# Transposed activations by DMA through HBM in place of TensorE transposes, in a convolution and FFN kernel

## The chip, the cores and the metric

The kernel runs on one core of one Trainium2 chip. The metric is device time in microseconds (us), the median of several runs. The engines are named as in the profile: PE is TensorE (PEld its weight loads), DVE is VectorE, ACT is ScalarE, POOL is GpSimd, SP is SyncE, whose queue here issues nearly all DMAs.

## The reference

A causal convolution of 7 taps over the sequence, with one softmax-normed set of taps for each of 8 groups of 24 channels, and then a gated feed-forward part without any nonlinearity: `a = y @ w1`, `b = y @ w2`, `out = ((a * b) @ w3) @ w_out`.

```python
B, S, D = x.shape            # 8, 3904, 192
w = softmax(weight)          # 8 heads x 7 taps
x_unf = x_pad[:, idx, :].reshape(B, S, K, H, group)
out = np.einsum('hk,bskhg->bshg', w, x_unf)
...
a = x @ w1                   # 31232 x 192 by 192 x 1024
b = x @ w2
h = a * b @ w3
return (h @ w_out).astype(np.float32)
```

## The kernel before

The 31232 tokens are cut in two ways. The convolution works on 32 **blocks** of 976 tokens (8 windows of 122). The products work on 61 **chunks** of 512 tokens.

For a block, `load_x` (L65) brings the rows of x as 128 partitions (122 rows and the 6 before them) by 8 windows. `cast_x` (L174) makes bf16 of them on GpSimd (`xb`). `conv_pair` (L187) multiplies with a band matrix per head on TensorE (L194, 8 matmuls per block into PSUM tiles `cps`), and ScalarE copies the results to `convo` (L198): 122 partitions are tokens, and channels lie along the free dimension. When the last pair of heads is done, GpSimd copies 64 channels once more within `convo` (L202), so that two groups of 128 columns are there: channels 0 to 127, and 128 to 191 twice.

The first product needs channels on partitions. `transp` (L210) does that on TensorE: 8 transposes of 122x128 for each of the two groups into a PSUM tile `tps` (L214), and VectorE copies to the **ring** (L219). The ring is three tiles `xT0`, `xT1`, `xT2` of 128 x 4096 in bf16 (8 chunks). `xT0` has channels 0 to 127, `xT2` channels 128 to 191 twice, and `xT1` the same channels as `xT0` with the halves exchanged, so that the products by `w1` (rows 0 to 63 of TensorE) and by `w2` (rows 64 to 127) both find each channel. For blocks 0 and 1 `xT1` is filled by copies of ScalarE and VectorE (L221, L222), from block 2 on by two DMAs on SyncE's queue that copy halves of `xT0` (L224, L225).

For a chunk, `first_product` (L262) makes for each of 8 column groups of the hidden layer two PSUM tiles `pa` and `pb` by 6 matmuls (L271, pairs of which run side by side on the two halves of the rows). ScalarE casts `pa` to `asb` (L276), VectorE multiplies it with `pb` to `abT` (L277). The weights w3 and w_out are multiplied beforehand into `W_sb` (`w3_cast`, `w3_transpose`, `w3_product`, L306 to L325), so that `second_product` (L281) is 16 matmuls for each half of a chunk (L290), an eviction to `osb` on ScalarE (L293) and a store on SyncE's queue (L295). It runs three chunks (`LAG`) behind.

The order of the work is the order of the program. Within the pair loop (L364) a pass takes two first products, and then four halves of second products, ahead of each of which one **step** of the convolution may stand: `band_products(it)` (the convolution of a block, the cast of the next block's x, the load of x three blocks ahead) or `transposes(it)`. The list `steps` (L242) says their order, and `steps_for` how many have to be done for a chunk; the loop looks `2 * PAIR` = 4 chunks ahead. Before the loop stands a prologue with the weights' preparation, the first three chunks and the first seven steps.

All PSUM tiles share 8 banks in turn. `xr` has 4 buffers, `xb`, `convo` and `osb` have 2.

Of the kernel before, what the change touches and what calls it, by code (L numbers as in the profile page):

```python
# [9 lines left out]
FP32 = mybir.dt.float32  # L10
BF16 = mybir.dt.bfloat16
# [6 lines left out]
def kernel(  # L18
# [10 lines left out]
    nc = tc.nc  # L29

    B, S, D = x.shape
# [3 lines left out]
    JT = DFF // 128  # L35
    PAD = K - 1

    ST = 122
    NW = 8
    BLK = ST * NW  # L40
    NB = B * S // BLK
    BPS = S // BLK
    CH = 512
    NCH = B * S // CH
    RING = 8 * CH
    LAG = 3
    PAIR = 2

    const = ctx.enter_context(tc.tile_pool(name="const", bufs=1))
    stage = ctx.enter_context(tc.tile_pool(name="stage", bufs=2))  # L50
    work = ctx.enter_context(tc.tile_pool(name="work", bufs=2))
    psum = ctx.enter_context(tc.tile_pool(name="psum", bufs=8, space=bass.MemoryType.PSUM))
    ctx.enter_context(tc.manual_schedule())

    def bank(shape, dtype, name):
        return psum.tile(shape, dtype, tag="bank", name=name)
# [50 lines left out]
    w3f = []  # L107
    for jt in range(JT):
# [11 lines left out]
        out=dmask, in_=ones.unsqueeze(2).to_broadcast([128, K, ST]),  # L120
# [9 lines left out]
    for q, (c0, j0, n) in enumerate(QC):  # L130
# [6 lines left out]
        out=wsb, in0=wsb, in1=wmax.unsqueeze(2).to_broadcast([128, H, K]),  # L137
# [6 lines left out]
        out=wsb, in0=wsb, in1=wsum.unsqueeze(2).to_broadcast([128, H, K]),  # L144
# [24 lines left out]
    xT0 = const.tile([128, RING], BF16)  # L169
    xT1 = const.tile([128, RING], BF16)  # L170
    xT2 = const.tile([128, RING], BF16)
    xT = (xT0, xT1, xT2)

    def cast_x(it, first=False):  # L174
        xb = work.tile([128, NW, D], BF16, tag="xb", bufs=2, name="xb")
        xr = xr_of.pop(it)
        if first:
            nc.scalar.copy(out=xb[:, 0:NW // 2, :], in_=xr[:, 0:NW // 2, :])
            nc.gpsimd.tensor_copy(out=xb[:, NW // 2:NW, :], in_=xr[:, NW // 2:NW, :])  # L179
        else:  # L180
            nc.gpsimd.tensor_copy(out=xb, in_=xr)  # L181
        return xb

    convo_of = {}
    xb_of = {}

    def conv_pair(it, t):  # L187
        if t == 0:
            convo_of[it] = work.tile([128, NW, D + 64], BF16, tag="convo", bufs=2, name="convo")
        convo, xb = convo_of[it], xb_of[it]  # L190
        cps = bank([128, 2, NW, G], FP32, "cps")
        for r in range(2):
            h = 2 * t + r
            nc.tensor.matmul(  # L194
                cps[0:ST, r], Aband[:, h, :], xb[:, :, h * G:(h + 1) * G],
                start=True, stop=True)
        dst = convo[0:ST, :, 2 * t * G:(2 * t + 2) * G]
        nc.scalar.copy(  # L198
            out=dst.rearrange("s b (r g) -> s r b g", r=2), in_=cps[0:ST])
        if t == 3:  # L200
            del xb_of[it]
            nc.gpsimd.tensor_copy(out=convo[0:ST, :, D:D + 64], in_=convo[0:ST, :, 128:192])  # L202

    def ring_spans(t0, n):
        a = t0 % RING
        if a + n <= RING:
            return [(0, a, n)]
        return [(0, a, RING - a), (RING - a, 0, n - (RING - a))]

    def transp(it, k):  # L210
        convo = convo_of[it]
        tps = bank([128, BLK], BF16, "tps")
        for w in range(NW):
            nc.tensor.transpose(  # L214
                out=tps[:, w * ST:(w + 1) * ST],
                in_=convo[0:ST, w, 128 * k:128 * (k + 1)],
                identity=ident[0:ST, 0:ST])
        for src, a, n in ring_spans(it * BLK, BLK):
            nc.vector.tensor_copy(out=xT[2 * k][:, a:a + n], in_=tps[:, src:src + n])  # L219
            if k == 0 and it < 2:  # L220
                nc.scalar.copy(out=xT1[0:64, a:a + n], in_=tps[64:128, src:src + n])  # L221
                nc.vector.tensor_copy(out=xT1[64:128, a:a + n], in_=tps[0:64, src:src + n])  # L222
            elif k == 0:
                nc.sync.dma_start(out=xT1[0:64, a:a + n], in_=xT0[64:128, a:a + n])  # L224
                nc.sync.dma_start(out=xT1[64:128, a:a + n], in_=xT0[0:64, a:a + n])  # L225
        if k == 1:
            del convo_of[it]


    def band_products(it):  # L230
        for t in range(4):
            conv_pair(it, t)
        if it + 1 < NB:
            xb_of[it + 1] = cast_x(it + 1)
        if it + 3 < NB:
            xr_of[it + 3] = load_x(it + 3)

    def transposes(it):
        transp(it, 0)
        transp(it, 1)  # L240

    steps = [(band_products, 0), (transposes, 0), (band_products, 1)]  # L242
    ready = {0: 2}
    for it in range(1, NB):
        if it + 1 < NB:
            steps.append((band_products, it + 1))
        steps.append((transposes, it))
        ready[it] = len(steps)
    done = [0]

    def conv_step():
        f, it = steps[done[0]]
        done[0] += 1
        f(it)

    def steps_for(c):
        return ready[(min((c + 1) * CH, B * S) - 1) // BLK]
# [4 lines left out]
    def first_product(c):  # L262
        ab = work.tile([128, JT, CH], BF16, tag="abT", bufs=LAG + 2, name="abT")
        abT_of[c] = ab
        r0 = (c * CH) % RING
        for ft in range(JT):
            pa = bank([128, CH], FP32, "pa")
            pb = bank([128, CH], FP32, "pb")
            for k in range(3):
                for dst, rows in ((pa, slice(0, 64)), (pb, slice(64, 128))):  # L270
                    nc.tensor.matmul(  # L271
                        dst, wb[k][rows, ft * 128:(ft + 1) * 128],
                        xT[k][rows, r0:r0 + CH],
                        start=(k == 0), stop=(k == 2))
            asb = work.tile([128, CH], BF16, tag="asb", bufs=4, name="asb")
            nc.scalar.copy(out=asb, in_=pa)  # L276
            nc.vector.tensor_tensor(out=ab[:, ft, :], in0=asb, in1=pb, op=ALU.mult)  # L277

    osb_of = {}

    def second_product(c, half):  # L281
        ab = abT_of[c]
        if half == 0:
            osb_of[c] = work.tile([128, 4, D], FP32, tag="osb", bufs=2, name="osb")
        osb = osb_of[c]
        ops = bank([128, 2, D], FP32, "ops")
        for r in range(2):
            g = 2 * half + r
            for jt in range(JT):
                nc.tensor.matmul(  # L290
                    ops[:, r, :], ab[:, jt, g * 128:(g + 1) * 128], W_sb[:, jt, :],
                    start=(jt == 0), stop=(jt == JT - 1))
        nc.scalar.copy(out=osb[:, 2 * half:2 * half + 2, :], in_=ops)  # L293
        if half == 1:
            nc.sync.dma_start(  # L295
                out=o_rows[c * CH:(c + 1) * CH, :].rearrange("(g p) d -> p g d", p=128),
                in_=osb)
            del osb_of[c], abT_of[c]
# [35 lines left out]

    bands(0)
    xb_of[0] = cast_x(0, first=True)
    bands(1)
    cast_w(0, (nc.scalar.copy, nc.scalar.copy, nc.gpsimd.tensor_copy))
# [25 lines left out]
    for c in range(LAG, NCH, PAIR):  # L364
        pair = range(c, min(c + PAIR, NCH))
        for cc in pair:
            first_product(cc)
        need = steps_for(min(c + 2 * PAIR, NCH - 1))
        for cc in pair:
            for half in range(2):  # L370
                if done[0] < need:
                    conv_step()
                second_product(cc - LAG, half)
        while done[0] < need:
            conv_step()
    for c in range(NCH - LAG, NCH):
        second_product(c, 0)
        second_product(c, 1)
# [30 lines left out]
```

## Time and profile before

| | us |
|---|---|
| median of 3 runs (lowest, highest) | 580.78 (580.12, 580.98) |
| the profiled execution | 580.07 |
| its span, first to last instruction | 578.4 |
| TensorE busy | 551.8 |
| ScalarE busy | 405.9 |
| VectorE busy | 373.7 |
| GpSimd busy | 79.0 |

The granted clock of TensorE was 0.997 of full speed over the span. A profile row of section 5 of the page names line, engine, operation, written and read tiles, count, busy time and mean duration, and the idle time before them with what ended it. The chain is followed back from the last instruction to whatever released each step. Matmuls are pipelined, so their single durations overlap and the chain's pieces say what one costs.

### The profile page before, as it was taken

How to read it: one execution, taken by the hardware profiler on the slowest of the kernel's cores; microseconds unless marked ns; L12 is line 12 of the kernel's file. 1: busy time of each engine (PE TensorE's matmuls, PEld its weight loads, DVE VectorE, ACT ScalarE, POOL GpSimd, SP SyncE). 2: the span in 40 equal slices, each digit the busy share in tenths (PEclk: the TensorE clock that was granted, in tenths of full speed). 3: DMA queues.
4: the chain of work that ended last, by engine and by line, in shares of the span. 5: the costliest groups of instructions: out<-in, count | busy, mean ns of one | idle time of the engine just before them, and what ended most of it. 6: DMA issues, size and time to landing. Idle time of an engine off the chain costs nothing.

```text
span 578.4 us, 14554 instructions
## 1 busy us (share of the span) xinstructions
PE 551.8 (95%) x5776; PEld 362.1 (63%) x5776; DVE 373.7 (65%) x590; ACT 405.9 (70%) x761; POOL 79.0 (14%) x94
## 2 busy tenths in 40 slices
PE   0869999999999999999999999999999999999997
PEld 0446576655666655666655666656666556666657
DVE  6447756776666776666776666776667866667770
ACT  2567777787777787777787777876777877776772
POOL 3352021100111100111100111111111101100000
PEclk9989999999999999999999999999999999999999
DMA  8992062334432334442334442364423322221014
GB/s 203 347 286 74 1 185 84 97 91 128 129 110 83 95 97 127 129 113 74 84 113 128 127 111 72 93 181 127 128 71 97 89 73 73 73 70 50 30 55 138
DMA packets 74793, 64.17 MB, mean 111 GB/s; under 512 B 3690, under 2 KB 72932, under 8 KB 74724
## 3 DMA queue, kind: packets, MB, share of 16 engines
q1 hardware_dynamic: 74100, 62.42, 37.5%
q10 hardware_dynamic: 624, 0.82, 0.6%
q8 instruction: 45, 0.74, 0.5%
q14 instruction: 24, 0.20, 0.1%
HBM read 31.74 MB, written 23.99 MB: 96 GB/s over the span
## 4 chain that ended last, share of the span: by engine, by line
PE 91%; issue 3%; DVE 2%; POOL 2%; ACT 1%; DMA 1%; ACTq 0%; POOLq 0%; DVEq 0%
PE pa L271 52%; PE ops L290 27%; PE tps L214 4%; PE cps L194 4%; PE pb L271 1%; PE wps L323 1%; POOL xb L181 1%; DMA xr<-in_x_dram 1%; DVE abT L277 1%; PE w3ps L314 0%; ACT convo L198 0%; POOL wb L333 0%; DVE cprod L153 0%; ACT w3b L308 0%; DVE xT L219 0%
## 5 line engine op out<-in xcount | busy, mean ns | idle before, releaser
L277 DVE TENSOR_TENSOR abT<-asb,pb 128x512 bf16<-128x512 bf16 x488 | 317.0, 688 | 130.4 <-PE pb L271 125.3
L271 PE MATMUL pa<-xT,wb 64*128 64x512 bf16 x1464 | 325.5, 378 | 1.1 <-ACT xT L221 0.6
L271 PE MATMUL pb<-xT,wb 64*128 64x512 bf16 x1464 | 325.5, 378 | 0.6 <-DVE xT L222 0.3
L276 ACT CAST asb<-pa 128x512 bf16<-128x512 f32 x488 | 285.7, 587 | 41.7 <-PE pb L271 14.1
L271 PEld LDWEIGHTS <-wb 64*128 64x128 bf16 x2928 | 141.6, 94 | 176.2 <-issue 13.4
L290 PE MATMUL ops<-W_sb,abT 128*128 128x192 bf16 x1952 | 170.8, 246 | 0.0
L290 PEld LDWEIGHTS <-abT 128*128 128x128 bf16 x1952 | 161.0, 98 | 0.8 <-issue 0.8
L293 ACT COPY osb<-ops 128x384 f32<-128x384 f32 x122 | 58.4, 479 | 104.4 <-PE ops L290 103.9
L202 POOL COPY convo<-convo 122x512 bf16<-122x512 bf16 x32 | 19.7, 615 | 414.6 <-ACT convo L198 398.9
L219 DVE COPY xT<-tps 128x976 bf16<-128x976 bf16 (+7 forms) x78 | 40.7, 570 | 48.0 <-PE tps L214 47.9
L198 ACT CAST convo<-cps 122x384 bf16<-122x384 f32 x128 | 52.3, 502 | 2.7 <-PE cps L194 2.7
L194 PE MATMUL cps<-xb,Aband 128*122 128x192 bf16 x256 | 29.1, 258 | 18.2 <-POOL xb L179 14.7
L181 POOL CAST xb<-xr 128x1536 bf16<-128x1536 f32 x31 | 45.6, 1470 | 0.0
L194 PEld LDWEIGHTS <-Aband 128*122 128x122 bf16 x256 | 23.1, 138 | 30.5 <-issue 16.4
L214 PE MATMUL tps<-ident,convo 122*128 122x122 bf16 x512 | 34.4, 222 | 1.4 <-ACT convo L198 1.3
L214 PEld LDWEIGHTS <-convo 122*128 122x128 bf16 x512 | 31.0, 101 | 2.4 <-ACT convo L198 1.6
L323 PE MATMUL wps<-wo_b,w3T 128*128 128x192 bf16 x64 | 6.6, 246 | 1.2 <-DVE w3T L317 1.1
L317 DVE COPY w3T<-w3ps 128x1024 bf16<-128x1024 bf16 x8 | 5.4, 690 | 2.9 <-PE w3ps L314 2.9
L325 ACT CAST W_sb<-wps 128x192 bf16<-128x192 f32 x8 | 2.6, 320 | 6.2 <-PE wps L323 6.2
L323 PEld LDWEIGHTS <-w3T 128*128 128x128 bf16 x64 | 5.1, 98 | 1.6 <-DVE w3T L317 1.6
L166 ACT COPY Aband<-cband 32x152 bf16<-32x152 bf16 (+1 forms) x4 | 1.2, 305 | 5.9 <-DVE cband L159 5.9
L139 ACT ACT_TABLE_LOAD x1 | 1.3, 1283 | 5.7 <-DMA xr<-in_x_dram 5.7
(36 smaller groups left out, 44.3 us busy)
## 6 DMA issues: line engine op xcount, KB each, us to landing
xr<-in_x_dram SPq DMA_DIRECT2D x31, 768.0 KB, 5.7
out_dram<-osb SPq DMA_DIRECT2D x61, 384.0 KB, 2.9
xT<-xT SPq DMA_DIRECT2D x46, 122.0 KB, 2.3
w3f<-in_moe_w_dram SPq DMA_DIRECT2D x8, 512.0 KB, 9.7
wo_f<-in_moe_w_out_dram SPq DMA_DIRECT2D x1, 768.0 KB, 9.7
xr<-in_x_dram SPq DMA_DIRECT2D x1, 672.0 KB, 6.6
w0f<-in_moe_w_dram ACTq DMA_DIRECT2D x2, 128.0 KB, 5.3
w1f<-in_moe_w_dram ACTq DMA_DIRECT2D x2, 128.0 KB, 6.2
```

Of the source, the lines that this page charges most:

```text
L181: nc.gpsimd.tensor_copy(out=xb, in_=xr)
L194: nc.tensor.matmul(cps[0:ST, r], Aband[:, h, :], xb[:, :, h * G:(h + 1) * G], start=True, stop=True)
L198: nc.scalar.copy(out=dst.rearrange("s b (r g) -> s r b g", r=2), in_=cps[0:ST])
L202: nc.gpsimd.tensor_copy(out=convo[0:ST, :, D:D + 64], in_=convo[0:ST, :, 128:192])
L214: nc.tensor.transpose(out=tps[:, w * ST:(w + 1) * ST], in_=convo[0:ST, w, 128 * k:128 * (k + 1)], identity=ident[0:ST, 0:ST])
L219: nc.vector.tensor_copy(out=xT[2 * k][:, a:a + n], in_=tps[:, src:src + n])
L271: nc.tensor.matmul(dst, wb[k][rows, ft * 128:(ft + 1) * 128], xT[k][rows, r0:r0 + CH], start=(k == 0), stop=(k == 2))
L276: nc.scalar.copy(out=asb, in_=pa)
L277: nc.vector.tensor_tensor(out=ab[:, ft, :], in0=asb, in1=pb, op=ALU.mult)
L290: nc.tensor.matmul(ops[:, r, :], ab[:, jt, g * 128:(g + 1) * 128], W_sb[:, jt, :], start=(jt == 0), stop=(jt == JT - 1))
L293: nc.scalar.copy(out=osb[:, 2 * half:2 * half + 2, :], in_=ops)
L323: nc.tensor.matmul(wps, w3T[:, gt, :], wo_b[:, gt, :], start=(gt == 0), stop=(gt == JT - 1))
```

## The change

From block 2 on (`PE_BLOCKS = 2`) TensorE no longer transposes. `convo` gets 384 columns: after the copy that was there, GpSimd makes two more, so that the three groups of 128 columns are what `xT0`, `xT2` and `xT1` hold. The rows of the block are stored to a buffer `rows` in HBM (three buffers) by two DMAs, of 112 and of 10 partitions. The step `transposes(it)` is then three transposing DMAs from `rows`, one per ring tile (twice three where the block wraps around the end of the ring), all on SyncE's queue. The copies L219, L224 and L225 are gone for these blocks. In `steps`, a block's `transposes` now comes right behind its `band_products`, and the loop looks 6 chunks ahead instead of 4. The output tile `osb` moves into the 8 buffers that the raw w3 weights used in the prologue.

```diff
+    dram = ctx.enter_context(tc.tile_pool(name="dram", bufs=3, space=bass.MemoryType.DRAM))
...
+    PE_BLOCKS = 2
+    C = 2 * D
...
-            convo_of[it] = work.tile([128, NW, D + 64], BF16, tag="convo", bufs=2, name="convo")
+            convo_of[it] = work.tile([128, NW, C], BF16, tag="convo", bufs=2, name="convo")
...
             nc.gpsimd.tensor_copy(out=convo[0:ST, :, D:D + 64], in_=convo[0:ST, :, 128:192])
+            if it >= PE_BLOCKS:
+                nc.gpsimd.tensor_copy(out=convo[0:ST, :, 256:320], in_=convo[0:ST, :, 64:128])
+                nc.gpsimd.tensor_copy(out=convo[0:ST, :, 320:384], in_=convo[0:ST, :, 0:64])
+                rows = dram.tile([NW, ST, C], BF16, tag="rows", bufs=3, name="rows")
+                rows_of[it] = rows
+                for a, b in ((0, 112), (112, ST)):
+                    nc.sync.dma_start(out=rows[:, a:b, :].rearrange("w s c -> s w c"),
+                                      in_=convo[a:b])
+                del convo_of[it]
...
-            if k == 0 and it < 2:
+            if k == 0:
...
-            elif k == 0:
-                nc.sync.dma_start(out=xT1[0:64, a:a + n], in_=xT0[64:128, a:a + n])
-                nc.sync.dma_start(out=xT1[64:128, a:a + n], in_=xT0[0:64, a:a + n])
...
     def transposes(it):
+        if it >= PE_BLOCKS:
+            rows = rows_of.pop(it).rearrange("w s c -> (w s) c")
+            for src, a, n in ring_spans(it * BLK, BLK):
+                for piece, dst in enumerate((xT0, xT2, xT1)):
+                    nc.sync.dma_start_transpose(
+                        out=dst[:, a:a + n],
+                        in_=rows[src:src + n, piece * 128:(piece + 1) * 128])
+            return
...
-    steps = [(band_products, 0), (transposes, 0), (band_products, 1)]
-    ready = {0: 2}
-    for it in range(1, NB):
-        if it + 1 < NB:
-            steps.append((band_products, it + 1))
+    steps = [(band_products, 0), (transposes, 0), (band_products, 1), (band_products, 2),
+             (transposes, 1), (transposes, 2)]
+    ready = {0: 2, 1: 5, 2: 6}
+    for it in range(3, NB):
+        steps.append((band_products, it))
         steps.append((transposes, it))
...
-            osb_of[c] = work.tile([128, 4, D], FP32, tag="osb", bufs=2, name="osb")
+            osb_of[c] = stage.tile([128, 4, D], FP32, tag="w3f", bufs=JT, name="osb")
...
-        need = steps_for(min(c + 2 * PAIR, NCH - 1))
+        need = steps_for(min(c + 3 * PAIR, NCH - 1))
```

On SyncE's queue, in a pass of the pair loop in which the block wraps around the end of the ring, there stands before (xT_140 and xT_141 are `xT0` and `xT1`):

```order
L77 DMA xr<-in_x_dram 128x8x192
L224 DMA xT_141<-xT_140 64x384
L225 DMA xT_141<-xT_140 64x384
L224 DMA xT_141<-xT_140 64x592
L225 DMA xT_141<-xT_140 64x592
L295 DMA out_dram<-osb 128x4x192 x2
```

and in the changed kernel (xT_142, xT_143 and xT_144 are `xT0`, `xT1` and `xT2`):

```order
L214 DMA rows<-convo 112x8x384
L214 DMA rows<-convo 10x8x384
L78 DMA xr<-in_x_dram 128x8x192
L254 DMA_TRANSPOSE xT_142<-rows 128x384
L254 DMA_TRANSPOSE xT_144<-rows 128x384
L254 DMA_TRANSPOSE xT_143<-rows 128x384
L254 DMA_TRANSPOSE xT_142<-rows 128x592
L254 DMA_TRANSPOSE xT_144<-rows 128x592
L254 DMA_TRANSPOSE xT_143<-rows 128x592
L314 DMA out_dram<-osb 128x4x192 x2
```

The stores of the rows come ahead of the load of x, and the transposing DMAs stand between it and the two stores of the output.

On GpSimd's queue, at block 2 in the prologue (a block's copies and the cast of the next x stand in this order for every later block, too), there stands before:

```order
L82 MEMSET xr 6x192
L202 COPY convo<-convo 122x8x64
L181 CAST xb<-xr 128x1536
L348 CAST wo_b<-wo_f 128x1536
L308 CAST w3b<-w3f 128x1024 x2
```

and in the changed kernel:

```order
L83 MEMSET xr 6x192
L207 COPY convo<-convo 122x8x64
L209 COPY convo<-convo 122x8x64
L210 COPY convo<-convo 122x8x64
L185 CAST xb<-xr 128x1536
L367 CAST wo_b<-wo_f 128x1536
L327 CAST w3b<-w3f 128x1024 x2
```

The two new copies stand ahead of the cast of the next block's x.

More of the change, by code (lines that the diff above doesn't have):

```diff
@@ L184 @@
     convo_of = {}
+    rows_of = {}
     xb_of = {}
```

## The prediction, made before the changed kernel was run

> **What bounds the kernel now.** I read the page's head first: the engines, the slices of the span, the chain that ended last.
>
> ```profile
> span 578.4 us, 14554 instructions
> PE 551.8 (95%) x5776; PEld 362.1 (63%) x5776; DVE 373.7 (65%) x590; ACT 405.9 (70%) x761; POOL 79.0 (14%) x94
> GB/s 203 347 286 74 1 185 84 97 91 128 129 110 83 95 97 127 129 113 74 84 113 128 127 111 72 93 181 127 128 71 97 89 73 73 73 70 50 30 55 138
> PE 91%; issue 3%; DVE 2%; POOL 2%; ACT 1%; DMA 1%; ACTq 0%; POOLq 0%; DVEq 0%
> PE pa L271 52%; PE ops L290 27%; PE tps L214 4%; PE cps L194 4%; PE pb L271 1%; PE wps L323 1%; POOL xb L181 1%; DMA xr<-in_x_dram 1%; DVE abT L277 1%; PE w3ps L314 0%; ACT convo L198 0%; POOL wb L333 0%; DVE cprod L153 0%; ACT w3b L308 0%; DVE xT L219 0%
> ```
>
> TensorE carries 91% of the chain and the transposes (tps, L214) alone 4%, which is about 23 us. So work taken off TensorE is worth its time until something else is late. Next the steady state: two passes of the pair loop in the windows view (engine busy, clock, DMA share, GB/s), one with a load of x and one without.
>
> ```profile
> 301.24:318.65 17.41, 17.41 (x188) 11.38 (x186) 11.64 (x19) 12.83 (x25) 2.03 (x2) 1.00 0.38 107
> 459.63:477.03 17.40, 17.40 (x186) 11.37 (x185) 11.63 (x19) 12.82 (x25) 2.03 (x2) 1.00 0.22 62
> ```
>
> TensorE is busy for the whole pass, ScalarE for 12.8 us of it, VectorE 11.6. The pass lasts 17.40 us at 62 and at 107 GB/s of DMA alike: DMA traffic does not slow the matmuls at these rates. Last, the chain inside one pass.
>
> ```profile
> 301.24 1.32 PE ops L290 x16
> 302.56 0.85 PE tps L214 x16
> 303.42 3.96 PE ops L290 x48
> ```
>
> The 16 transposes of a block stand between two stretches of the second product and fill the chain from 302.56 to 303.42, 0.855 us.
>
> **Part 1: transposes leave TensorE.** Blocks 2 to 31 lose theirs: 30 x 0.855 = 25.65 us off the path. Two places give some back.
>
> The first is block 2, in the prologue. The chain between 43 and 64 us, summed by line, reads:
>
> ```profile
> by line: PE wps L323 23.7%; DVE abT L277 16.3%; issue 13.0%; PE w3ps L314 12.8%; PE pa L271 12.4%; ACT w3b L308 6.6%; DVE w3T L317 6.3%; ACT convo L198 4.7%; ACT asb L276 2.4%; PE cps L194 2.3%; PE pb L271 0.4%; DVEq L277 0.1%
> ```
>
> ScalarE and VectorE share the path there and the transposes are not on it, so block 2's are worth between 0 and 0.85 us. I take half: 0.45 back.
>
> **Part 2: two more copies on GpSimd, ahead of the cast of x.** Each block gets two copies of 122x512 behind the one it has, and the cast to xb for the next block comes after all three. In a pass with one block nobody notices: the next block's matmuls are a pass away. The pair loop runs ahead by 1024 tokens a pass and a block has 976, so in two passes (the first, and before 300 to 400 us) two blocks fall in one pass. Before, such a pass looks like this (timeline: start, duration):
>
> ```profile
> 369.99 0.87 PE L194 MATMUL cps<-xb,Aband 128*122 128x192 bf16 x8
> 372.34 0.62 POOL L202 COPY convo<-convo 122x512 bf16<-122x512 bf16 x1 [15.19 <-ACT convo L198]
> 372.89 1.48 POOL L181 CAST xb<-xr 128x1536 bf16<-128x1536 f32 x1
> 374.42 0.82 PE L194 MATMUL cps<-xb,Aband 128*122 128x192 bf16 x8
> ```
>
> The second block's matmuls start as the cast ends: convolution to convolution 4.43 us, GpSimd and TensorE almost level. GpSimd repeats copies of 128x512 at this spacing:
>
> ```profile
> 20.03 0.61 POOL L333 CAST wb<-w0f 128x512 bf16<-128x512 f32 x1
> 20.59 0.61 POOL L333 CAST wb<-w1f 128x512 bf16<-128x512 f32 x1
> 21.14 0.61 POOL L333 CAST wb<-w2f 128x512 bf16<-128x512 f32 x1
> ```
>
> That is 0.56 us each, so xb comes 1.1 us later, while TensorE arrives 0.855 us sooner for want of the transposes: a wait of 1.95 us, twice, 3.9 us back. Bounds: 0 (the copies hide) to 2 x (0.855 + 2 x 0.62) = 4.2.
>
> **Part 3: what the others lose.** VectorE loses two copies to the ring per block. Its busy time in a pass falls from 11.6 to about 10.4 us, of a pass of 16.55. It is off the path, so nothing is counted. The PSUM banks come round with two fewer takers per block, and their evictions stay far ahead of TensorE: nothing.
>
> **Part 4: SyncE's queue.** Per block it loses two ring copies and gains two stores of rows (750 KB together, 976 packets of 768 bytes, about a load of x) and three transposing DMAs (six where the ring wraps). The first of these waits for the rows to land. Behind it stand two stores of the output and the next block's rows and load of x. The trace has the landing of such sizes (KB each, us from issue to landing) and the queue's spare time:
>
> ```profile
> out_dram<-osb SPq DMA_DIRECT2D x61, 384.0 KB, 2.9
> xr<-in_x_dram SPq DMA_DIRECT2D x31, 768.0 KB, 5.7
> SPq L224 <- DVE xT L219: 357.3, 30, 28.4
> ```
>
> So the queue stands for some 6 us per pass, where today it stands 357 us in all at one line. The output stores then come 6 us late, and osb has 8 buffers in place of 2. Loads of x are three blocks ahead. The ring's free place is given by the first products that TensorE has just ended in the same pass, so that wait costs nothing; and block 6, for one, made in the pass of chunks 5 and 6, is first read by chunk 11. That leaves over two passes, 33 us, of cover for the round trip. If the round trip were over 33 us, its excess would be paid in each pass.
>
> **Part 5: the sixteen DMA engines.** This term decides. In the pass at 301.24 us the DMA view says:
>
> ```profile
> DMA packets 2259, 1.86 MB, mean 107 GB/s; under 512 B 80, under 2 KB 2256, under 8 KB 2256
> q1 hardware_dynamic: 2256, 1.82, 37.4%
> ```
>
> One packet costs an engine 0.374 x 17.41 us x 16 / 2256 = 46.2 ns, at 807 bytes on average. A block will need 1024 packets for x, 976 for rows, 976 for the output and 128 for semaphores: 3104, or 8.96 us on 16 engines. The three transposes read 3 x 976 pieces of 256 bytes, 183 per engine. The trace has no transposing DMA. Lower bound of a piece: its bytes at the best slice of the page, 347 GB/s, which is 11.8 ns, 2.2 us per block. Upper bound from the nearest row: a plain packet's 46.2 ns, 8.45 us. I take the middle, 29 ns or 5.3 us, since a piece carries a third of a packet's bytes: 14.3 us of DMA in a pass of 16.55. It fits, under TensorE's cover, and costs nothing.
>
> The Trainium skill (DMA: Bandwidth & Descriptors, Latency and other measured facts) gives 261 GB/s as the measured rate of transposing DMAs with a strided middle dimension; by that a block's 750 KB would be an estimated 2.9 us, near the lower bound, and the sum stays as it is. No row here shows it.
>
> **The sum.** 580.07 us (the profiled execution; its span is 578.4) - 25.65 + 0.45 + 3.9 = 558.8 us. The runs' median of 580.78 lies 0.7 us above that execution, so on its scale 559.5 us. With all bounds 554 to 566.
>
> **The rivals.**
>
> A. *The DMA engines become the bound (slower).* Place: every pass. If a block's DMA work D exceeds the pass, the kernel goes at D: the first transposes can start when block 2's rows have landed, 30 blocks follow, and then the last first products and what comes after them.
>
> ```profile
> 37.41 0.60 POOL L202 COPY convo<-convo 122x512 bf16<-122x512 bf16 x1
> 550.47 0.39 PE L271 MATMUL pa<-xT,wb 64*128 64x512 bf16 x1
> ```
>
> Block 2's copies would end at 37.41 + 0.60 + 1.1 = 39.1 us, the rows land near 43. From chunk 59's first product to the end are 578.4 - 550.5 = 28 us; 1.7 us lie outside the span. Time = 72.7 + 30 D. At 46.2 ns a piece D = 17.4 and the time 595 us. It is worse than before from D = 16.9 on, which is 43.4 ns a piece. For it: the bound from the nearest row lies just beyond that point. Against it: pieces are a third of the packets' size, and at the 347 GB/s of slice 2 even a packet of 768 bytes takes an engine 35 ns. Chance 0.10.
>
> B. *Transposing is slower than copying, by tile.* The crossing of rows and columns costs the engines time of its own. With two plain packets per piece, 92.4 ns, D = 25.9 and the time 849 us; each further 46 ns adds 254. For it: no row excludes it; each piece of 256 bytes must be scattered over 128 partitions. Against it: nothing either, in this trace. Chance 0.17. The Trainium skill (VectorE: DVE Perf Modes, The three transpose paths) gives 1309 ns for a 128x128 transpose by DMA; a block is 22.9 such squares, and if they went one after another that is an estimated 29.9 us per block, some 970 us by the formula. The same skill's other rate, above, speaks against it, and no run here shows either.
>
> C. *The time comes back as another wait.* Say the cast of x is late in every pass, or the transposing writes disturb TensorE's reads: at 1.95 us lost a pass over 28 passes it would all be gone, at half of that the time is near 573 us. Against it: the windows above, with equal passes at 62 and 107 GB/s, and a cast that has most of a pass to spare. Chance 0.08.
>
> **How the numbers follow.** Forecast 0.62, C 0.08, A 0.10, B 0.17, and 0.03 for landing within 0.2% of before, which is about what a measurement of this kernel can tell from no change. Faster: 0.62 + 0.08 = 0.70; same 0.03; slower 0.27. The range starts at the lower bound of the sum, 553, and reaches over C and to the middle of A, 600; B and what is left of A stay outside, some 0.2.
>
> **What would show it.** Right: passes of about 16.55 us with TensorE busy throughout, no L214 matmul after the prologue's two blocks, waits for xb of about 2 us in two passes only, DMA share below 0.9 in a pass. Wrong: TensorE waiting at L271 for xT, a DMA share near 1, transposes landing later than 33 us after their issue, and passes longer than 17.4 us (A, B); or a TensorE idle in each pass that is not for xT (C).

## The result and the profile after

| | before | after |
|---|---|---|
| median, us | 580.45 | 559.65 (559.08 to 560.12) |
| ratio | | 0.9643, 95% interval 0.963 to 0.9656 |
| profiled execution, its span, us | 580.07, 578.4 | 559.08, 557.3 |

The forecast was 559.5 us. First the head of the page after, with the busy times, the DMA slices, the DMA queue and the chain:

```profile
span 557.3 us, 13715 instructions
PE 526.0 (94%) x5296; PEld 336.5 (60%) x5296; DVE 335.8 (60%) x516; ACT 405.9 (73%) x761; POOL 112.6 (20%) x154
DMA  7979339997977769767788787998778893665114
q1 hardware_dynamic: 189632, 99.91, 73.3%
PE 82%; issue 2%; POOL 1%; ACT 0%
```

TensorE has 25.8 us less work and is still the bound. The DMA queue went from 37.5% to 73.3% of its sixteen engines, and DMA is not on the chain as far as the page follows it, which is back to 77 us, 86% of the span. The steady passes, in the windows view (length, then busy time of PE, PEld, DVE, ACT and POOL, clock, DMA share, GB/s), and thirteen passes in one window:

```profile
290.36:306.91 16.55, 16.55 (x169) 10.52 (x170) 10.40 (x17) 12.82 (x24) 3.15 (x4) 1.00 0.76 188
306.91:323.46 16.55, 16.55 (x169) 10.52 (x170) 10.40 (x17) 12.82 (x24) 3.15 (x4) 1.00 0.83 159
108.33:323.46 215.13, 215.13 (x2186) 136.71 (x2186) 135.21 (x209) 166.72 (x312) 41.65 (x55) 1.00 0.81 193
```

A pass lasts 16.55 us instead of 17.40, and TensorE is busy in all of it. VectorE's busy time fell from 11.6 to 10.40 us. The chain within one pass shows where the 0.855 us went: the second product's 64 matmuls now stand in one piece behind the convolution's eight.

```profile
306.91 0.80 PE cps L199 x8
307.71 5.28 PE ops L309 x64
```

Now the pass with two blocks, in the timeline, with the idle time ahead of an instruction and what ended it in brackets:

```profile
339.94 0.87 PE L199 MATMUL cps<-xb,Aband 128*122 128x192 bf16 x8
342.28 0.62 POOL L207 COPY convo<-convo 122x512 bf16<-122x512 bf16 x1 [13.40 <-issue]
342.83 0.62 POOL L209 COPY convo<-convo 122x512 bf16<-122x512 bf16 x1
343.39 0.62 POOL L210 COPY convo<-convo 122x512 bf16<-122x512 bf16 x1
343.95 1.47 POOL L185 CAST xb<-xr 128x1536 bf16<-128x1536 f32 x1
345.47 0.82 PE L199 MATMUL cps<-xb,Aband 128*122 128x192 bf16 x8 [2.03 <-POOL xb L185]
```

The copies follow each other every 0.56 us, the cast starts 1.1 us later than it did, and TensorE waits 2.03 us. The first pass of the loop has the same, 2.05 us:

```profile
79.18 0.82 PE L199 MATMUL cps<-xb,Aband 128*122 128x192 bf16 x8 [2.05 <-POOL xb L185]
```

And SyncE's queue in one pass:

```profile
294.39 0.88 SPq L214 DMA_DIRECT2D rows<-convo  x2
295.31 1.42 SPq L78 DMA_DIRECT2D xr<-in_x_dram  x1
299.39 4.04 SPq L254 DMA_TRANSPOSE xT<-rows  x3
303.54 1.07 SPq L314 DMA_DIRECT2D out_dram<-osb  x2
```

The convolution starts at 290.36, the rows are stored from 294.39, and the transposing DMAs are issued when the rows have landed, from 299.39 to 303.4. TensorE waits for none of that.

### The profile page after: what moved, and what is told of

It reads as the page before. It is cut to its first block, busy times and chain, and to the rows that moved or that the text cites. A ratio compares the mean times of both kernels' runs of the same rounds, so it can differ in the third digit from the quotient of the medians.

```text
span 557.3 us, 13715 instructions
## 1 busy us (share of the span) xinstructions
PE 526.0 (94%) x5296; PEld 336.5 (60%) x5296; DVE 335.8 (60%) x516; ACT 405.9 (73%) x761; POOL 112.6 (20%) x154
## 3 DMA queue, kind: packets, MB, share of 16 engines
q1 hardware_dynamic: 189632, 99.91, 73.3%
## 4 chain that ended last, share of the span: by engine, by line
PE 82%; issue 2%; POOL 1%; ACT 0%
PE pa L290 50%; PE ops L309 27%; PE cps L199 4%; PE pb L290 1%; POOL xb L185 1%; POOL convo L210 0%; POOL convo L209 0%; ACT osb L312 0%; POOL convo L207 0%
## 5 line engine op out<-in xcount | busy, mean ns | idle before, releaser
L309 PE MATMUL ops<-W_sb,abT 128*128 128x192 bf16 x1952 | 166.3, 246 | 0.0
L207 POOL COPY convo<-convo 122x512 bf16<-122x512 bf16 x32 | 19.7, 615 | 317.3 <-issue 256.9
L210 POOL COPY convo<-convo 122x512 bf16<-122x512 bf16 x30 | 18.5, 616 | 0.0
L209 POOL COPY convo<-convo 122x512 bf16<-122x512 bf16 x30 | 18.5, 616 | 0.0
L83 POOL MEMSET xr<- 6x192 f32 x7 | 1.7, 249 | 53.6 <-DMA xr<-in_x_dram 53.6
L233 DVE COPY xT<-tps 128x976 bf16<-128x976 bf16 x4 | 2.7, 667 | 9.4 <-PE tps L228 9.3
```

What stands on the lines that cost most here:

```text
L209: nc.gpsimd.tensor_copy(out=convo[0:ST, :, 256:320], in_=convo[0:ST, :, 64:128])
L210: nc.gpsimd.tensor_copy(out=convo[0:ST, :, 320:384], in_=convo[0:ST, :, 0:64])
L309: nc.tensor.matmul(ops[:, r, :], ab[:, jt, g * 128:(g + 1) * 128], W_sb[:, jt, :], start=(jt == 0), stop=(jt == JT - 1))
```

## The experiments

The theory after the result: TensorE's missing transposes are the whole gain, the round trip through HBM is covered, and only GpSimd's longer work ahead of the cast gives something back. The rivals: part of the gain is the new order of the steps or the buffers; the DMA traffic costs something after all; the cover was never needed. Ratios are to the kernel before, with their 95% interval.

**Cast first.** One part undone: GpSimd casts the next block's x ahead of the three copies.

```diff
...
         if it + 1 < NB:
             xb_of[it + 1] = cast_x(it + 1)
+        if it >= PE_BLOCKS:
+            store_rows(it)
```

The new function `store_rows` holds the three copies and the two stores that stood in `conv_pair`.

> One thing is undone in the changed kernel (559.65 us): GpSimd casts the next block's x before it makes the three copies of a block's rows, as it did before the two new copies came in. Theory: in two passes of the pair loop TensorE waits 2.03 and 2.05 us for that cast, and this is all that the longer GpSimd work costs; with the cast first both waits go and the time is 555.6 us (555.0 to 556.2). The rows reach HBM 1.5 us later, which the look-ahead covers. Rival: the waits are not on the path (another wait takes their place), time 559 to 560 us. Second rival: the later rows are missed somewhere, time above 560 us.

Measured: 554.92 us, ratio 0.9569 (0.9554 to 0.9585), 4.3 us less than the change by the difference of the ratios. The pass with two blocks now goes through without a stop:

```profile
337.92 0.87 PE L199 MATMUL cps<-xb,Aband 128*122 128x192 bf16 x8
340.25 0.61 POOL L212 COPY convo<-convo 122x512 bf16<-122x512 bf16 x1 [13.41 <-issue]
341.26 0.82 PE L199 MATMUL cps<-xb,Aband 128*122 128x192 bf16 x8
```

From convolution to convolution it is 3.34 us, against 5.53 in the change, and no wait is left. The theory holds, a little beyond its interval. This is the fastest version of the study.

**The order alone.** The change without its DMAs: transposes on TensorE for all blocks, the ring filled as before, but the new order, look-ahead and buffers.

```diff
-    PE_BLOCKS = 2
-    C = 2 * D
+    PE_BLOCKS = NB
+    C = D + 64
...
```

The rest of the edit puts back the two DMAs that copy halves of `xT0`.

> The change without its DMAs: the new order of steps, the look-ahead of 6 chunks and the 8 output buffers stay, but all blocks are transposed on TensorE and the ring is filled as before. Theory: the gain is TensorE work taken away and nothing else, so this stands at the time before, 580.5 us (579 to 582). Rival: part of the gain is the earlier order or the buffers; then it is clearly below, for instance 570 us.

Measured: 597.08 us, ratio 1.0281 (1.0264 to 1.0298): slower than before, which neither side had expected. Windows and timeline of one pass:

```profile
292.44:310.42 17.98, 17.58 (x185) 11.38 (x186) 11.74 (x19) 12.82 (x24) 2.21 (x3) 1.00 0.36 103
294.39 0.59 PE L228 MATMUL tps<-ident,convo 122*128 122x122 bf16 x8
294.72 0.61 POOL L207 COPY convo<-convo 122x512 bf16<-122x512 bf16 x1 [15.95 <-ACT convo L203]
295.39 0.60 PE L228 MATMUL tps<-ident,convo 122*128 122x122 bf16 x8 [0.40 <-POOL convo L207]
```

A block's transposes now stand one half of a second product behind its own convolution, and TensorE runs into ScalarE's and GpSimd's work on that block. The pass is 17.98 us, 0.58 longer than before, and 28 such passes make 16 us. So the order, the look-ahead and the buffers bring no gain of their own; the order does no harm in the change only because the step that stands there has no TensorE instruction in it.

**No round trip.** From block 6 on the rows are neither stored nor transposed.

```diff
-                for a, b in ((0, 112), (112, ST)):
+                for a, b in ((0, 112), (112, ST)) if it < 6 else ():
...
+        if it >= 6:
+            return
```

> The changed kernel without the stores of the rows and the transposing DMAs from block 6 on; the ring then holds old data, and GpSimd's copies stay. Theory: the round trip is wholly under TensorE's cover, so leaving it out gains nothing: 559.6 us (559 to 560.2), with the two waits for the cast of x still there. Rival: the DMA traffic slows TensorE or its partners by some per cent of the pass; then this is 2 to 10 us faster.

Measured: 560.55 us, ratio 0.9654 (0.9641 to 0.9666), the same as the change within the intervals. The DMA queue drops and the time stays:

```profile
span 558.1 us, 13442 instructions
DMA  7979338933312233322233332333312211111104
```

So the traffic of the round trip costs nothing that these runs can tell, neither as waiting nor as contention.

**Four chunks ahead.** The change with the old look-ahead.

```diff
-        need = steps_for(min(c + 3 * PAIR, NCH - 1))
+        need = steps_for(min(c + 2 * PAIR, NCH - 1))
```

> The changed kernel with the look-ahead of the loop set back from 6 chunks to the 4 that it was before. Theory: the round trip from a block's convolution to the landing of its third transpose takes about 15.6 us, and it is the longer look-ahead that hides it. With 4 chunks, eleven blocks (11 to 21) are first read by the second product pair's second chunk of the very next pass, 11.3 us after their convolution began, so each of these passes waits about 4 us: 604 us (590 to 615). For all other blocks the cover is 22 us or more and nothing changes. Rival: the round trip is shorter than 11 us, and the time stays at 559.6 us.

Measured: 616.22 us, ratio 1.0609 (1.0585 to 1.0634), so 56.6 us more than the change. TensorE waits for the ring in ten passes, twice in each, not in the eleven that were expected (total, times, longest):

```profile
PE pa L290 <- DMA xT<-rows: 37.5, 20, 3.9
```

That is 3.75 us in each of the ten passes, near the 4 that were expected, but a pass loses 5.7. One of them in the windows view, and the stretch of its waits in the timeline:

```profile
255.64:277.27 21.63, 18.35 (x170) 11.14 (x170) 10.52 (x18) 12.81 (x24) 3.14 (x4) 0.92 0.59 144
269.05 0.39 PE L290 MATMUL pa<-xT,wb 64*128 64x512 bf16 x1 [2.04 <-DMA xT<-rows]
270.68 0.58 PE L290 MATMUL pa<-xT,wb 64*128 64x512 bf16 x1 [1.24 <-DMA xT<-rows]
271.06 0.63 PE L290 MATMUL pa<-xT,wb 64*128 64x512 bf16 x1
271.49 0.63 PE L290 MATMUL pa<-xT,wb 64*128 64x512 bf16 x1
```

The two waits are 3.3 us, and behind them matmuls come every 0.43 us instead of every 0.215 for some 3 us; the clock granted over the pass was 0.92. The Trainium skill (TensorE: Matmul & The Clock Gate, Why this matters for your kernels) says that gaps over about 3 us throw the clock back to half. Neither gap here is that long: two gaps of 2.04 and 1.24 us close together did it, while the single wait of 2.03 us in the change left the clock at 1.00, as this window of it shows:

```profile
339.90:356.50 16.60, 14.57 (x154) 10.12 (x154) 7.61 (x13) 11.90 (x25) 6.47 (x9) 1.00 0.89 221
```

So the look-ahead is what hides the round trip, and a late transfer costs more than its lateness: 37.5 us of waits, and some 19 us more that go with the slower clock behind them, 1.8 us in the pass shown.

**Each transposing DMA twice, and three times.** The extra ones write to spare memory.

```diff
...
+                for more in range(1):
+                    for piece in range(3):
+                        nc.sync.dma_start_transpose(
+                            out=spare[piece][:, more, src:src + n],
+                            in_=rows[src:src + n, piece * 128:(piece + 1) * 128])
```

The second kernel has `range(2)` in place of `range(1)`.

> The changed kernel with every transposing DMA issued a second time into spare memory that nobody reads. Theory: a piece of 256 bytes costs an engine 23 ns (the stretch of the changed kernel's trace from 56.3 to 60.7 us), so the second set adds 2976 packets x 23.0 / 16 = 4.3 us to the 12.4 us of DMA work per pass: 16.6 us, level with TensorE's 16.55. By the prediction's formula 72.7 + 30 D that is 572 us; expected 560 to 580, the DMA share near 1 and TensorE beginning to wait for the ring. Rival 1: TensorE's cover still holds, 559.6 us. Rival 2: transposing DMAs get in each other's way, well above 580.

> The changed kernel with every transposing DMA issued three times, the second and third into spare memory. Theory: 12.4 + 2 x 4.3 = 20.9 us of DMA work per block, so the DMA engines set the pace: 72.7 + 30 x 20.9 = 700 us (670 to 730), DMA share near 1. Rival 1: the pace is SyncE's, which spends 1.25 us on issuing each transposing DMA: 9 x 1.25, 3.4 for the other issues and 2.5 of waiting for the rows make 17.2 us per block, 589 us. Rival 2: nothing of it is on the path, 559.6 us.

Measured: 622.2 us, ratio 1.0727 (1.0698 to 1.0756), and 762.08 us, ratio 1.312 (1.3076 to 1.3164). Both are slower than the theory had it, by 50 and 62 us. To see where, take SyncE's queue in rounds, from one block's store of rows to the next. Two rounds of the doubled kernel in the windows view, a plain one and one whose block wraps around the end of the ring:

```profile
264.40:281.30 16.90, 16.90 (x168) 10.54 (x166) 9.87 (x16) 12.29 (x25) 3.14 (x4) 0.97 1.06 222
298.90:323.60 24.70, 24.70 (x260) 17.07 (x256) 14.75 (x23) 18.96 (x37) 3.14 (x4) 1.00 0.75 157
```

and two of the tripled one:

```profile
339.30:360.30 21.00, 18.00 (x184) 11.90 (x183) 11.13 (x18) 13.94 (x28) 3.14 (x4) 1.00 1.06 216
360.30:393.10 32.80, 27.87 (x269) 17.40 (x266) 15.74 (x24) 19.82 (x38) 3.14 (x4) 0.95 0.62 145
```

A block that wraps transposes the same rows with twice the DMAs, 12 and 18 in place of 6 and 9. Its round is 7.8 and 11.8 us longer, which is 1.3 us for each DMA more, and the DMA engines' share falls to 0.75 and 0.62. So in these rounds SyncE's queue sets the pace and not the engines. It issues with hardly a pause but the 2.6 us in which it waits for the rows (L256 fills the ring, L261 the spare memory):

```profile
360.34 2.16 SPq L214 DMA_DIRECT2D rows<-convo  x2
362.55 2.17 SPq L78 DMA_DIRECT2D xr<-in_x_dram  x1
367.33 3.79 SPq L256 DMA_TRANSPOSE xT<-rows  x3
371.16 7.89 SPq L261 DMA_TRANSPOSE spare<-rows  x6
379.46 4.66 SPq L256 DMA_TRANSPOSE xT<-rows  x3
384.17 7.64 SPq L261 DMA_TRANSPOSE spare<-rows  x6
391.90 1.08 SPq L321 DMA_DIRECT2D out_dram<-osb  x2
```

In the plain rounds the engines' share is 1.06 (a share above 1 means that the times of packets overlap) and the queue has hardly a pause either, and in the doubled kernel's round shown here TensorE is busy throughout as well, so what sets the pace there isn't settled. By the starts of the stores in the traces a plain round from block 5 on lasts 16.8 us on average and a wrapping one 23.8 in the doubled kernel, 20.8 and 31.6 in the tripled one. With 23 plain and 7 wrapping rounds in place of the 30 D of the prediction's formula that makes 626 and 772 us, where 622 and 762 were measured. So the theory's 16.6 and 20.9 us hold for the plain rounds, and what it left out are the issues of the wrapping ones. The first rival of the second kernel, the pace of SyncE, had the right mechanism at too low a price: it counted 9 transposing DMAs to a block, where the mean is 11.1.

What a further set costs the engines can be read from the pages: the queue's packets take 73.3, 87.5 and 88.4% of spans of 557.3, 623.8 and 759.8 us, so the extra sets add 137 and 126 us, or 4.6 and 4.2 us per block. That is near the theory's 4.3, so the second rival of the first kernel, transposes in each other's way, isn't needed. TensorE waits for what the queue brings late, the ring and x.

**The new copies on VectorE.**

```diff
-                nc.gpsimd.tensor_copy(out=convo[0:ST, :, 256:320], in_=convo[0:ST, :, 64:128])
-                nc.gpsimd.tensor_copy(out=convo[0:ST, :, 320:384], in_=convo[0:ST, :, 0:64])
+                nc.vector.tensor_copy(out=convo[0:ST, :, 256:320], in_=convo[0:ST, :, 64:128])
+                nc.vector.tensor_copy(out=convo[0:ST, :, 320:384], in_=convo[0:ST, :, 0:64])
```

> The changed kernel with its two new copies on VectorE in place of GpSimd; the old copy and the cast of x stay on GpSimd in the old order. Theory: what counts is only what stands ahead of the cast of x on GpSimd, so the two waits of 2 us shrink by the 1.1 us that the copies took, to 0.9 us each, because TensorE still comes 0.855 us sooner than before: 557.4 us (556.8 to 558.2). Rival: VectorE has the copies in its path (it stands behind the product of each chunk), and the time is 559.6 us or more.

Measured: 557.92 us, ratio 0.961 (0.9597 to 0.9623), and the wait in the pass with two blocks is the 0.9 us that was left for it:

```profile
342.59 0.29 DVE L209 COPY convo<-convo 122x512 bf16<-122x512 bf16 x1 [0.52 <-ACT convo L203]
345.08 0.82 PE L199 MATMUL cps<-xb,Aband 128*122 128x192 bf16 x8 [0.91 <-POOL xb L185]
```

So what is given back is the work ahead of the cast: the wait follows it to within 0.1 us.

## Why the prediction was right

**The 25.65 us.** Passes of 16.55 us were forecast and measured. Leaving the round trip out altogether changes nothing, so the gain is TensorE's missing work alone. That the step's new place would cost nothing was right only because no TensorE instruction stands in it any more: with one there, the same order costs 16 us. The prediction had not looked at that.

**Block 2 in the prologue, taken at half.** It was the lower bound, nothing. The convolution of block 2 and the first matmul of chunk 3 before:

```profile
33.21 1.44 PE L194 MATMUL cps<-xb,Aband 128*122 128x192 bf16 x8 [3.48 <-POOL xb L181]
61.97 0.39 PE L271 MATMUL pa<-xT,wb 64*128 64x512 bf16 x1
```

and after:

```profile
33.11 1.12 PE L199 MATMUL cps<-xb,Aband 128*122 128x192 bf16 x6 [3.48 <-POOL xb L185]
61.87 0.39 PE L290 MATMUL pa<-xT,wb 64*128 64x512 bf16 x1
```

Both are 0.10 us earlier, so the transposes between them were worth nothing, and the gain is 29 x 0.855 = 24.8 us.

**GpSimd's longer work: 1.95 us, twice.** Measured 2.03 and 2.05. With them 24.8 - 4.1 = 20.7 us, where 21.3 were forecast; the spans differ by 21.1, of which 0.1 is that earlier start, and the other 0.3 is not traced. So the terms hold to some tenths of a microsecond, and the agreement of 559.5 with 559.65 is closer than that by luck. Of the stated bounds, 554 follows from the terms, but 566 does not: block 2 at 0.85 and two waits of 2.1 make 559.5, or 560.2 on the medians' scale, and no term is named for the rest. The 553 at which the range starts is not that 554 either.

**The sixteen engines, 29 ns a piece and 14.3 us in a pass.** A stretch in which nearly only transposes run, while block 3's are on their way, reads in the DMA view:

```profile
GB/s 154 168 177 165 137 56 16 19 16 19 114 277 291 291 262 284 296 289 293 289 286 289 101 93 100 77 95 140 189 242 265 291 293 231 168 56 0 0 0 0
DMA packets 2861, 0.72 MB, mean 163 GB/s; under 512 B 2841, under 2 KB 2861, under 8 KB 2861
q1 hardware_dynamic: 2861, 0.72, 93.5%
```

From 56.3 to 60.7 us that is 0.935 x 4.4 us x 16 / 2861 = 23.0 ns a piece, half of a plain packet; the pages' shares above give 25.0 and 22.9. The 29 ns were the middle of two far bounds, taken for want of a row, and that they came near is luck; but any price below the 43.4 ns of rival A would have left the time as it is. The pass needs 13.4 us by the share of 0.81 over thirteen passes (the 12.4 us of the expectations came from a single one), so some 3 us were free, and a second set uses them up.

Rivals A and B fail by their price of a piece. The rule of the Trainium skill beside B (VectorE: DVE Perf Modes, The three transpose paths; 1309 ns for a 128x128 square) fails with them if the squares go one after another: a block's 22.9 squares would take an estimated 29.9 us by it, and a further set of them took 4.2 to 4.6 us of the engines' time. The skill's other rate, 261 GB/s (DMA: Bandwidth & Descriptors, Latency and other measured facts), is not decided here: the stretch above ran at 163 on average, with slices of 16 to 19 GB/s in it and others of up to 296.

The prediction did not price the issue of the transposing DMAs; it had SyncE's queue stand for some 6 us in a pass. In the pass shown above the queue is taken from 294.39 to 304.61, 10.2 us, and TensorE covers that, too. It was this queue that gave way in the wrapping rounds of the doubled kernel, with the engines at 0.75.

**The cover.** The prediction put it at two passes, 33 us. The run with four chunks ahead shows that cover is needed: with 11.3 us of it TensorE waited 3.75 us on average, so the round trip takes some 15 us.

**Rival C** fell: the only waits that came back are the two for the cast. Its price was wrong, too: 1.95 us over 28 passes is 54.6 us, more than twice the gain, and the 573 us stand for a quarter of it.

## What to carry to other kernels

Work that leaves the bounding engine is worth its place in the chain, and a slower path for it costs nothing as long as its throughput fits and its latency is looked ahead for; test both, by doubling the new transfers and by shortening the look-ahead. Count the issues of the new transfers as well as their bytes: doubling them doubles both, and in the doubled and tripled kernels here it was the issuing queue that was full in the rounds that cost most. What is added on an idle engine is still late for whoever waits behind it in that engine's queue: put it behind the instruction that the bounding engine waits for. A reordering that comes with a change is to be costed with the change's own instructions in it, as the same order may cost or be free by what stands there.

## What the runs showed of the hardware

SyncE spent about 1.25 us on issuing one transposing DMA (1.115 at the least), against 0.49 for a store of rows (minimum, median and maximum in ns):

```profile
L254 SPq DMA_TRANSPOSE xT<-rows x111: 1115/1246/2771, 44.3 to 503.2; - x111
L214 SPq DMA_DIRECT2D rows<-convo x60: 317/489/1808, 39.4 to 496.2; - x60
```

The time goes by the DMA and not by its rows: in the wrapping round above, where each DMA has a part of a block, six took 7.89 and 7.64 us to issue, and in the plain round before it six for a whole block took 7.98.

A VectorE copy of 122x512 in bf16 took 0.29 us where GpSimd took 0.62. And TensorE's matmuls came at half their rate for some 3 us after waits of 2.04 and 1.24 us that ended 1.6 us apart, while a single wait of 2.03 us left the clock at 1.00.
